# Loading a decode kernel's small inputs as three rows on a second queue, spread by small matrix products

## The chip, the cores and the metric

The kernel runs on one core of one Trainium2 chip. Times are microseconds (us) of device time. An execution's time is about 1.8 us longer than the span in its profile.

Terms: PE is the matrix engine and PEld its weight load; DVE the vector engine, ACT the scalar engine, POOL the GpSimd engine, SP the sync engine. SPq and ACTq are the queues on which SP and ACT issue DMA transfers. The work of a transfer is done by 16 DMA engines, in packets.

## The reference, cut to what matters

```python
x = A_x                                             # [2, 1, 1024], bf16
g = sigmoid((x * gate_w).sum(-1, keepdims=True))    # gate_w: [1024]
q = (x @ wq).reshape(2, 1, 32, 128)                 # wq: 1024 x 4096, 8 MB
a = softmax(q @ k_cache^T / sqrt(128)) @ v_cache    # 2 x 32 heads, 16384 positions, Dh = 128
a = a.reshape(2, 1, 4096) @ wo
b = mixer_mlp(x)                                    # LayerNorm, w1, w2, w3, w4
return g * a + (1 - g) * b
```

The K and V caches are 537 MB of the 572.5 MB that are read. x is 4 KB and gate_w 2 KB.

## The kernel before

Transfers of 8 MB go through three large buffers in the order wq, K0, K1, V0, K2, V1 and so on. A load is issued when the buffer three loads back has been read. So K0 and K1 are issued at once, and V0 when PE has finished with wq. All of them are on SP's queue, x and gate_w behind wq:

```python
    x_pm = const.tile([P, B, KC], BF16)       # P = 128, B = 2, KC = 8
    gw_pm = const.tile([P, KC], BF16)

    def load_first():
        load_rows(["wq"], [A_wq])
        with nc.allow_non_contiguous_dma(reason="a few KB"):
            nc.sync.dma_start(out=x_pm[:], in_=A_x.rearrange("b s (p r) -> p (b s) r", p=P))
            nc.sync.dma_start(out=gw_pm[:], in_=gate_w.rearrange("(p r) -> p r", p=P))
```

In this form a partition gets 8 neighbouring elements of each row, 16 bytes: 256 pieces for x and 128 for gate_w. The query is computed by 64 products, in whose first step x must be in the transposed layout xT:

```python
    def compute_q():
        nc.vector.tensor_copy(out=xT[:], in_=x_pm[:].rearrange("p b r -> p r b"))
        wq = wt.pop("wq")
        ...
                    nc.tensor.matmul(ps[group(g), :], lhsT=xT[:, r, :],
                                     rhs=wq[:, r, c0 : c0 + CW], ...)
        ...
    steps = [("q", compute_q), ("gate", compute_gate)]     # then K0, K1, V0 ...
```

For a K tile, DVE transposes 16 times and PE makes four products after each transpose. The products need z, which is made from q; the transposes do not, but only two of their buffers exist.

## Time and profile before

| | kernel before |
|---|---|
| median of the first 3 executions | 1334.93 us |
| span of the profiled execution | 1333.6 us |
| PE, DVE, ACT busy | 60%, 57%, 2% |
| share of the 16 DMA engines' span taken by SP's queue | 99.4% |

The page of the kernel before, its slices (tenths busy in 40 equal slices of the span) and its queue table (packets, MB, share of 16 engines' span):

```profile
DMA  9999999999999999999999999999999999999998
...
q1 hardware_dynamic: 12729, 572.54, 99.4%
```

The DMA engines are never seen idle for long: q1 is SP's queue, and it fills them. They bound the kernel.

The timeline of the kernel before, its start (start us, us, engine, line, operation, output<-input, count, and in brackets the idle time before it and what ended that):

```profile
0.73 0.38 SPq L159 DMA_DIRECT2D wt<-in_A_wq_dram  x1
1.18 0.41 SPq L185 DMA_DIRECT2D x_pm<-in_A_x_dram  x1
1.63 0.47 SPq L186 DMA_DIRECT2D gw_pm<-in_gate_w_dram  x1
2.14 1.02 SPq L108 DMA_DIRECT2D Kn<-in_A_k_cache_dram  x2
22.81 0.18 DVE L299 COPY xT<-x_pm 128x16 bf16<-128x16 bf16 x1 [19.39 <-DMA x_pm<-in_A_x_dram]
23.04 5.79 PE L311 MATMUL misc<-wt,xT 128*2 128x512 bf16 x64 [19.56 <-DVE xT L299]
28.88 0.33 SPq L119 DMA_DIRECT2D Vn<-in_A_v_cache_dram  x1
43.60 2.37 DVE L369 STREAM_TRANSPOSE T<-Kn 128x1024 f32<-128x1024 f32 x2 [12.45 <-DMA Kn<-in_A_k_cache_dram]
```

Read the brackets. PE stands 19.56 us before the first product and waits for xT, which waits for x, which lies behind wq. The last line shows what follows: once q is done, DVE stands 12.45 us more, because K0 has not landed. It could help only the line before it, V0's issue at 28.88; and V0 has K1 ahead of it in the queue until about 61 us.

### The profile page before, as it was taken

Reading aid. Unit: us, or ns where it says so; the run is one execution under the profiler, and the core shown is the slowest. Engines: PE = TensorE matmul, PEld = TensorE weight load, DVE = VectorE, ACT = ScalarE, POOL = GpSimd, SP = SyncE. Lnnn points to the kernel's source line nnn. Section 1 sums busy time; section 2 is a strip of 40 time slices with the busy share of each in tenths; the row PEclk is TensorE's granted clock in tenths of the full one; section 3 lists DMA queues with packets and bytes.
Section 4 is the critical chain, followed back from the end, with each engine's and each line's share of the span. In section 5 each row is a group of like instructions: output and inputs, shape, how many; then the busy total and the mean of one; then the engine's idle time right before and its main releaser. Section 6 shows DMA issues by size and latency. Waiting matters only on the chain.

```text
span 1333.6 us, 11483 instructions
## 1 busy us (share of the span) xinstructions
PE 797.4 (60%) x4974; PEld 351.3 (26%) x5037; DVE 760.1 (57%) x999; ACT 27.2 (2%) x68; POOL 12.8 (1%) x40
## 2 busy tenths in 40 slices
PE   2576655766556755556665555576655556665564
PEld 0223222322225322222222222232222222222231
DVE  1677665466653665555666555566655556665540
ACT  0000000000000000000000000000000000000000
POOL 0000000000000000000000000000000000000000
PEclk9788777787777777788887777888777788877775
DMA  9999999999999999999999999999999999999998
GB/s 410 437 439 417 439 431 437 423 433 433 438 432 435 429 427 439 439 437 427 429 437 431 439 431 439 429 431 437 429 435 433 439 431 429 435 432 437 429 422 338
DMA packets 12787, 573.27 MB, mean 430 GB/s; under 512 B 1797, under 2 KB 1805, under 8 KB 2613
## 3 DMA queue, kind: packets, MB, share of 16 engines
q1 hardware_dynamic: 12729, 572.54, 99.4%
q8 instruction: 39, 0.64, 0.2%
q14 instruction: 11, 0.09, 0.0%
q10 hardware_dynamic: 8, 0.00, 0.0%
HBM read 572.53 MB, written 0.00 MB: 429 GB/s over the span
## 4 chain that ended last, share of the span: by engine, by line
DVE 30%; PE 30%; DMA 23%; another core or an unknown queue 12%; issue 2%; ACT 1%; SPq 0%; ACTq 0%
DVE T L369 24%; PE S L383 19%; DMA Kn<-in_A_k_cache_dram 13%; PE O L427 7%; DMA wt<-in_B_w_dram 4%; DMA Vn<-in_A_v_cache_dram 3%; DMA wo<-in_A_wo_dram 3%; PE misc L254 2%; DVE Os L442 2%; ACT Pr L411 1%; DVE PT L415 1%; PE misc L585 1%; DVE mx L404 1%; PE misc L566 1%
## 5 line engine op out<-in xcount | busy, mean ns | idle before, releaser
L383 PE MATMUL S<-T,z 128*128 128x512 bf16 x1985 | 579.8, 419 | 330.1 <-DVE T L369 308.5
L369 DVE STREAM_TRANSPOSE T<-Kn 128x1024 f32<-128x1024 f32 x512 | 612.1, 1230 | 255.0 <-DMA Kn<-in_A_k_cache_dram 204.8
L383 PEld LDWEIGHTS <-z 128*128 128x128 bf16 x2048 | 210.0, 104 | 686.6 <-issue 522.8
L427 PE MATMUL O<-Vn,PT 128*32 128x512 bf16 x2048 | 121.4, 390 | 3.6 <-DMA Vn<-in_A_v_cache_dram 3.6
L427 PEld LDWEIGHTS <-PT 128*32 128x32 bf16 x2048 | 73.9, 141 | 49.9 <-issue 20.7
L438 DVE TENSOR_SCALAR Os<-O,xmask 128x128 f32<-128x128 f32 x32 | 11.2, 351 | 101.6 <-PE O L427 101.6
L254 PE MATMUL misc<-rs,ones_f 128*128 128x2 f32 x64 | 17.9, 349 | 79.1 <-DVE rs L458 79.1
L411 ACT ACTIVATE Pr<-S,nb 128x512 bf16<-128x512 f32 x32 | 22.0, 687 | 1199.6 <-DVE nb L406 1161.7
L394 DVE TENSOR_REDUCE m<-S 128x1 f32<-128x512 f32 x32 | 22.2, 693 | 36.9 <-PE S L383 36.9
L450 PE MATMUL misc<-asel,Os 128*128 128x2 f32 x64 | 12.2, 261 | 51.1 <-DVE Os L442 51.1
L415 DVE STREAM_TRANSPOSE PT<-Pr 128x512 bf16<-128x512 bf16 x32 | 22.8, 711 | 28.7 <-ACT Pr L411 28.7
L254 PEld LDWEIGHTS misc<-rs,ones_f 128*128 128x128 f32 x64 | 16.1, 312 | 84.0 <-issue 81.2
L442 DVE SCALAR_TENSOR_TENSOR Os<-O,xmask,Os 128x128 f32<-128x128 f32 x96 | 33.7, 351 | 3.4
L450 PEld LDWEIGHTS misc<-asel,Os 128*128 128x128 f32 x64 | 9.5, 188 | 65.3 <-DVE Os L442 61.0
L254 PE MATMUL misc<-mdiag,ones_f 128*128 128x128 f32 x64 | 15.5, 325 | 17.1 <-DVE mdiag L397 17.1
L404 DVE TENSOR_REDUCE mx<-misc 64x1 f32<-64x64 f32 x64 | 14.2, 222 | 19.1 <-PE misc L254 18.6
L343 POOL TENSOR_TENSOR z<-qsel,own 128x32 bf16<-128x32 bf16 x32 | 10.7, 335 | 1201.2 <-PE S L383 1171.4
L585 PE MATMUL misc<-xn2T,wt 128*128 128x2 bf16 x224 | 14.4, 202 | 7.3 <-DMA wt<-in_B_w_dram 7.3
L462 DVE RECIPROCAL rinv<-misc 128x2 f32<-128x2 f32 x32 | 5.5, 171 | 22.7 <-PE misc L254 22.7
L684 DVE CAST T<-out_acc 128x256 bf16<-128x256 f32 x1 | 0.4, 425 | 30.6 <-PE out_acc L476 30.6
L311 PE MATMUL misc<-wt,xT 128*2 128x512 bf16 x64 | 5.8, 541 | 19.6 <-DVE xT L299 19.6
L585 PEld LDWEIGHTS <-wt 128*128 128x128 bf16 x224 | 14.3, 172 | 7.5 <-DMA wt<-in_B_w_dram 7.5
(86 smaller groups left out, 117.7 us busy)
## 6 DMA issues: line engine op xcount, KB each, us to landing
Vn<-in_A_v_cache_dram SPq DMA_DIRECT2D x2, 4096.0 KB, 41.7
wt<-in_B_w_dram SPq DMA_DIRECT2D x1, 7168.0 KB
w<-in_B_w_dram SPq DMA_DIRECT2D x4, 1792.0 KB, 31.8
wo<-in_A_wo_dram SPq DMA_DIRECT2D x6, 1024.0 KB, 34.1
wt<-in_B_w_dram SPq DMA_DIRECT2D x1, 2048.0 KB, 37.6
wt<-in_B_w_dram SPq DMA_DIRECT2D x1, 1536.0 KB, 41.4
wo<-in_A_wo_dram SPq DMA_DIRECT2D x2, 512.0 KB, 18.8
wo<-in_A_wo_dram SPq DMA_DIRECT2D x4, 256.0 KB, 13.7
```

The lines of the kernel that those rows point to most:

```text
L254: nc.tensor.matmul(ps[:], lhsT=ones_f[:], rhs=src, start=True, stop=True)
L369: moved = nc.vector.transpose(out=T[:].rearrange("p w j s -> p j w s"), in_=Kw[:, m * CW : (m + 1) * CW].rearrange("p (j w e) -> p j w e", ...
L383: nc.tensor.matmul(S[:], lhsT=z[:, v, NM - 1 - m : NM - 1 - m + P], rhs=Tb[:, v // 2, :, v % 2], start=(m == 0 and v == 0), stop=(m == NM ...
L394: nc.vector.reduce_max(out=m[:], in_=S[:], axis=AX.X)
L404: nc.vector.reduce_max(out=mx[pa, :], in_=mall[pa, pa], axis=AX.X)
L411: nc.scalar.activation(out=Pr[:], in_=S[:], func=ACTF.Exp, bias=nb[:], scale=scale, accum_out=rs[:])
L415: nc.vector.transpose(out=PT[:], in_=Pr[:])
L427: nc.tensor.matmul(O[32 * g : 32 * g + 32, :], lhsT=PT[:, m : CJ * 32 : 16], rhs=V[:, j0 : j0 + 4, :], start=(m == 0), stop=(m == NM - 1),)
L442: nc.vector.scalar_tensor_tensor(out=Os[:], in0=Ox, scalar=xmask[:, x : x + 1], in1=Os[:], op0=ALU.mult, op1=ALU.add,)
L450: nc.tensor.matmul(oc[:], lhsT=Os[:], rhs=asel[:], start=True, stop=True)
L566: nc.tensor.matmul(ps[group(g), :], lhsT=actT[rows, r, :], rhs=w[rows, r, g * HW : (g + 1) * HW], start=False, stop=(n == len(slots) - 1), ...
L585: nc.tensor.matmul(ps[:, c, :], lhsT=w[:, r, :].rearrange("k (p c) -> k p c", c=C)[:, :, c], rhs=actT[:, r, :], start=(r == 0), stop=(r == ...
```

## The change

Its intent is to get x and gate_w early: as three long rows on ACT's own queue, not behind wq. A row lies in one partition, so eight small products with an identity spread it over 128 partitions; two DVE copies follow.

```diff
-    x_pm = const.tile([P, B, KC], BF16)
-    gw_pm = const.tile([P, KC], BF16)
+    x_in = []
     def load_first():
+        x_rows = t_tile([B + 1, D], BF16)
+        x_in.append(x_rows)
+        nc.scalar.dma_start(out=x_rows[0:B, :], in_=A_x.rearrange("b s d -> (b s) d"))
+        nc.scalar.dma_start(out=x_rows[B : B + 1, :], in_=gate_w.rearrange("(o d) -> o d", o=1))
         load_rows(["wq"], [A_wq])
-            nc.sync.dma_start(out=x_pm[:], in_=A_x.rearrange("b s (p r) -> p (b s) r", p=P))
-            nc.sync.dma_start(out=gw_pm[:], in_=gate_w.rearrange("(p r) -> p r", p=P))
...
+    def spread_x():
+        x_rows = x_in.pop()
+        xg_ps = misc_psum([P, KC, B + 1])
+        for r in range(KC):
+            nc.tensor.matmul(xg_ps[:, r, :], lhsT=x_rows[:, r:D:KC],
+                             rhs=ident_b[0 : B + 1, 0 : B + 1], start=True, stop=True)
+        nc.vector.tensor_copy(out=xg[:], in_=xg_ps[:])
+        nc.vector.tensor_copy(out=xT[:], in_=xg[:, :, 0:B])
...
-    steps = [("q", compute_q), ("gate", compute_gate)]
+    steps = [("", spread_x), ("q", compute_q), ("gate", compute_gate)]
```

(Cut: the 32-column bf16 identity, the gate's product reading xg, the removed copy in compute_q.)

More of the change, by code (lines that the diff above doesn't have):

```diff
@@ L175, in load_pieces @@
         wt[key] = t
-    x_pm = const.tile([P, B, KC], BF16)
-    gw_pm = const.tile([P, KC], BF16)
+    x_in = []
     def load_first():
+        x_rows = t_tile([B + 1, D], BF16)
+        x_in.append(x_rows)
+        nc.scalar.dma_start(out=x_rows[0:B, :], in_=A_x.rearrange("b s d -> (b s) d"))
+        nc.scalar.dma_start(out=x_rows[B : B + 1, :], in_=gate_w.rearrange("(o d) -> o d", o=1))
         load_rows(["wq"], [A_wq])
-        with nc.allow_non_contiguous_dma(reason="a few KB"):
-            nc.sync.dma_start(out=x_pm[:], in_=A_x.rearrange("b s (p r) -> p (b s) r", p=P))
-            nc.sync.dma_start(out=gw_pm[:], in_=gate_w.rearrange("(p r) -> p r", p=P))
     ident_f = const.tile([P, P], FP32)
@@ L198 @@
     nc.vector.memset(neg_half[:], -0.5)
+    ident_b = const.tile([P, 32], BF16)
+    nc.vector.tensor_copy(out=ident_b[:], in_=ident_f[:, 0:32])
     zero = const.tile([P, 1], BF16)
@@ L259, in over_r @@
         return v.unsqueeze(1).to_broadcast([P, KC, B])
+    xg = const.tile([P, KC, B + 1], FP32)
+    def spread_x():
+        x_rows = x_in.pop()
+        xg_ps = misc_psum([P, KC, B + 1])
+        for r in range(KC):
+            nc.tensor.matmul(
+                xg_ps[:, r, :],
+                lhsT=x_rows[:, r:D:KC],
+                rhs=ident_b[0 : B + 1, 0 : B + 1],
+                start=True,
+                stop=True,
+            )
+        nc.vector.tensor_copy(out=xg[:], in_=xg_ps[:])
+        nc.vector.tensor_copy(out=xT[:], in_=xg[:, :, 0:B])
     g_bc = const.tile([P, B], FP32)
@@ L267, in compute_gate @@
         nc.vector.tensor_tensor(
-            out=prod[:], in0=x_pm[:], in1=gw_pm[:].unsqueeze(1).to_broadcast([P, B, KC]), op=ALU.mult
+            out=prod[:],
+            in0=xg[:, :, 0:B].rearrange("p r b -> p b r"),
+            in1=xg[:, :, B].unsqueeze(1).to_broadcast([P, B, KC]),
+            op=ALU.mult,
         )
@@ L298, in compute_q @@
     def compute_q():
-        nc.vector.tensor_copy(out=xT[:], in_=x_pm[:].rearrange("p b r -> p r b"))
         wq = wt.pop("wq")
```

## The prediction

> **What bounds the kernel now.** The DMA engines. The page's slices show DMA 90% busy or more in 39 of 40; its queue table gives q1 (SyncE's) 99.4% of 16 engines' span for 572.54 MB; PE has 60%, DVE 57%. By the packet records a 64 KB packet takes 2.42 us and the next starts at once, from 1.7 us to about 1317; in the first 1300 us an engine is idle under 3 us in all. Computing waits for data: the groups table puts 204.8 us of DVE idle before the K transposes down to K's DMA.
>
> **The start, from the timeline.** SyncE issues wq at 0.73, x at 1.18, gate_w at 1.63, K0 and K1 from 2.14 us. x lies behind 8 MB of wq on the same rings, so xT is made at 22.81, q's first product runs at 23.04, the q work ends at 31.4; then all stands until K0 lands: DVE waits 12.45 us and starts on K0 at 43.60. V0, which needs wq's buffer, is issued at 28.88, with K1 queued until about 62.
>
> **Removed.** 384 DMA packets of 16 B, in the records in a row between wq and K0, about 9 ns each: 24 an engine, 0.21 us. The gaps between wq's last and K0's first 64 KB packet average 0.21 us too. This is on the critical resource. The wait for x goes as well: q can start when wq lands, at about 22.4 instead of 23.04.
>
> **Added.** Three rows of 2 KB on ScalarE's queue at the start (a 2 KB packet takes 0.085 us here), on the same 16 engines: the Trainium skill ("DMA: Bandwidth & Descriptors", section "Issuing engines are not separate DMA queues") says a second issuing engine interleaves on them and saves only issue time. By the same page's section on why a semaphore rises by 16, two rows use two engines; there I expect 0.1 to 0.2 us. Eight small PE products, a cast and two copies on DVE, roughly 2 us together (the like here take 0.1 to 0.4), at about 4 to 8 us, when PE and DVE have nothing else. ScalarE's table load comes a microsecond later; it is first used at 29.6.
>
> **On the critical path.** Of the earlier q nothing: K0 lands 12 us after the q work, V0 is queued 33 us early. Only the tiny packets' 0.2 us counts, less what the rows cost the slowest engine. wo's last pieces land at 1329.4, the kernel ends at 1333.6; engines finish between 1322 and 1329.4, so 0.1 us on one may vanish. PE gets 16 more instructions; a shifted instruction fetch (39 packets of 16 KB, 0.95 us each) could move the end by some tenths either way.
>
> **Predicted: 1334.7 us (0.2 less), 8 times in 10 between 1333.9 and 1335.5. Faster by over 2%: 0.01; within 2%: 0.98; slower by over 2%: 0.01.**
>
> **Right if** the tiny packets are gone; xT is ready before 8 us; q's first product comes at about 22.4, V0's issue at about 28.3; K0's first transpose moves only 0.2 us, to about 43.4, and DVE's wait before it grows past 13 us; q1 keeps over 99%; the last wo piece lands at about 1329.2.
> **Wrong if** wq's first packets start after 1.7 us because ScalarE's issues come first; wq still lands late; K0 moves over 0.5 us; gaps appear on the DMA engines.
>
> **What would make it wrong.** A start of the DMA queue that the second queue disturbs; an engine that falls behind and sets the end alone; a difference between chips, larger than the effect.

## The result

The changed kernel took 1334.94 us (median of 6, 1334.68 to 1335.15), the kernel before 1334.89 (median of 6, 1334.84 to 1335.04). The ratio is 1.000, with a 95% interval of 0.9987 to 1.0013. Ratios here are the mean time of one kernel's fast runs over that of the other's of the same rounds, so not quite the ratio of the medians.

The page of the changed kernel, the same lines (q10 is ACT's queue):

```profile
DMA  9999999999999999999999999999999999999998
...
q1 hardware_dynamic: 12313, 572.53, 99.4%
...
q10 hardware_dynamic: 14, 0.01, 0.0%
```

q1 lost 416 packets: the 384 of 16 B and their completions. Its share stays at 99.4%. The timeline of the changed kernel, its start:

```profile
0.73 0.39 SPq L159 DMA_DIRECT2D wt<-in_A_wq_dram  x1
0.74 0.56 ACTq L183 DMA_DIRECT2D T<-in_A_x_dram  x1
1.18 1.03 SPq L108 DMA_DIRECT2D Kn<-in_A_k_cache_dram  x2
1.33 0.24 ACTq L184 DMA_DIRECT2D T<-in_gate_w_dram  x1
10.23 0.63 PE L269 MATMUL misc<-ident_b,T 3*128 3x3 bf16 x8 [7.62 <-DMA T<-in_gate_w_dram]
11.12 0.17 DVE L277 CAST xT<-xg 128x16 bf16<-128x16 f32 x1
22.58 6.21 PE L330 MATMUL misc<-wt,xT 128*2 128x512 bf16 x64 [10.53 <-DMA wt<-in_A_wq_dram]
28.85 0.34 SPq L119 DMA_DIRECT2D Vn<-in_A_v_cache_dram  x1
43.22 2.37 DVE L388 STREAM_TRANSPOSE T<-Kn 128x1024 f32<-128x1024 f32 x2 [12.10 <-DMA Kn<-in_A_k_cache_dram]
```

xT is there 11.7 us earlier. PE's wait now ends with wq, not x, and the first product comes 0.46 us earlier. Yet the 64 products take 6.21 us instead of 5.79, and V0's issue has moved by 0.03 us. K0's first transpose has moved by 0.38 us (in a second pair of traces, below, by 0.16: 43.52 and 43.36; so part of it is chance).

Three questions were left. Did the removed packets gain anything? Why did V0's issue not move? And what were the rows and the second queue each for?

### The profile page after: what moved, and what is told of

It reads as the page before. It is cut to its first block, busy times and chain, and to the rows that moved or that the text cites. A ratio compares the mean times of both kernels' runs of the same rounds, so it can differ in the third digit from the quotient of the medians.

```text
span 1333.3 us, 11505 instructions
## 1 busy us (share of the span) xinstructions
PE 805.6 (60%) x4982; PEld 354.5 (27%) x5045; DVE 759.7 (57%) x1001; ACT 27.2 (2%) x68; POOL 12.8 (1%) x40
## 3 DMA queue, kind: packets, MB, share of 16 engines
q1 hardware_dynamic: 12313, 572.53, 99.4%
## 4 chain that ended last, share of the span: by engine, by line
PE 31%; DVE 30%; DMA 23%; another core or an unknown queue 12%; issue 2%; ACT 1%; ACTq 0%; SPq 0%; DVEq 0%
DVE T L388 23%; PE S L402 20%; DMA Kn<-in_A_k_cache_dram 13%; PE O L446 7%; DMA wt<-in_B_w_dram 4%; DMA Vn<-in_A_v_cache_dram 3%; DMA wo<-in_A_wo_dram 3%; PE misc L255 2%; DVE Os L461 2%; ACT Pr L430 1%; DVE PT L434 1%; PE misc L604 1%; PE misc L585 1%; DVE mx L423 1%
## 5 line engine op out<-in xcount | busy, mean ns | idle before, releaser
L469 PE MATMUL misc<-asel,Os 128*128 128x2 f32 x64 | 12.4, 264 | 50.9 <-DVE Os L461 50.9
L484 DVE SCALAR_TENSOR_TENSOR OT<-misc,g_bc,rinv 128x2 bf16<-128x2 f32 x32 | 7.0, 220 | 15.6 <-PE misc L469 15.6
```

What stands on the lines that cost most here:

```text
L469: nc.tensor.matmul(oc[:], lhsT=Os[:], rhs=asel[:], start=True, stop=True)
```

## The experiments

"Its kernel before" is the unchanged kernel on the same chip in the same rounds. Where two times are given as medians and their difference as a mean, the difference is of the means.

### The two kernels once more, and a kernel that loads nothing

The first two kernels are unchanged. The third has no loads of x and gate_w. Its output is wrong, which doesn't matter for the time.

```diff
         load_rows(["wq"], [A_wq])
-            nc.sync.dma_start(out=x_pm[:], in_=...)
-            nc.sync.dma_start(out=gw_pm[:], in_=...)
+        nc.vector.memset(x_pm[:], 0.05)
+        nc.vector.memset(gw_pm[:], 0.05)
```

> The kernel before, unchanged, to see how much two executions of one kernel differ, in time and in the trace. Both theories: ratio 1.000. Theory A (the two traces differ mostly by chance): its start of K0's first transpose lies anywhere from 43.2 to 43.7 us and wq's first packets take anywhere from 2.5 to 3.4 us each, so the 0.38 us by which K0 moved between the two traces is only partly the change. Theory B (the change gained all of it): 43.6 us again, within 0.1.

> The changed kernel again. Theory A (24 packets of 16 B an engine gone, on the resource that bounds all): 0.1 to 0.3 us faster than the kernel before, at the edge of what can be resolved. Theory B (nothing gained at all, the packets fit into time that was free): 0.0. Theory C (the gain is there and is given back at the end): K0's start earlier, the last wo piece not earlier.

> The kernel before with x and gate_w not loaded at all but set to a constant (a wrong result, on purpose): the most that any way of loading them can gain. Theory A: 0.1 to 0.3 us faster, no more than the changed kernel; q's first product at about 22.5 us, V0's issue at about 28.8. The intent of the change (an earlier q is worth something): over 0.5 us faster.

Times: the kernel before again 1335.14 (5 executions, 1334.94 to 1335.93), the changed kernel again 1334.98 (5), without the loads 1334.87 (5), their kernel before 1334.92 (9). So two groups of executions of the very same kernel before, on one chip, differ by 0.30 us in the mean (0.13 without the slowest execution, 1335.93). The changed kernel is 0.04 us below the one group and 0.34 below the other; without the loads it is 0.20 below the first (standard error 0.11). Differences under 0.3 us cannot be told from such times with confidence.

The traces tell more than the times here, because the start has few sources of scatter. From the records of single DMA packets, as means over the 16 engines, in us from the span's start (worked out from the traces; the last column is the one packet of wo that ends last):

```
                     wq's last packet   K0's first   K0's last    wo's last
                     ends               starts       ends         ends
before                    22.01           22.22        41.72       1329.40
before, again             21.93           22.22        41.83       1329.91
changed                   21.94           21.95        41.37       1329.04
changed, again            21.96           21.97        41.39       1329.03
no loads at all           21.91           21.92        41.33       1328.99
```

With the tiny packets there is a gap of 0.21 and 0.29 us between wq and K0, without them none. K0 is complete 0.40 us earlier in the changed kernel (mean of two against mean of two), and the changed kernel reaches what loading nothing reaches, within 0.05 us. Of the 0.40 us, 0.25 is the gap and 0.13 a slower transfer of K0 after it (19.56 against 19.43 us from first to last packet). That it is the packets and not the queue or the rows is supported by x_after_k0 below, where the same packets stand behind K0 on the same queue: K0 is complete at 41.28 (one trace). So the removed packets did cost something, on the resource that bounds, and on an average engine the change recovered it within 0.05 us. wo's column cannot be read in the same way. The two traced executions of the kernel before were among its slowest (1333.6 and 1334.1, where the other executions in these rounds had spans of 1333.0 to 1333.5), and in x_after_k0, which keeps the 24 packets, wo ends at 1328.95, as early as in the changed kernel. Over all executions, on several chips, the changed kernel's mean is 1334.92 (11) and the kernel before's 1335.05 (43): 0.13 us less, give or take 0.13 (two standard errors), but that mixes chips; in the rounds of the result the changed kernel's mean was 0.02 us more (standard error 0.07). So the times do not settle even the sign.

### Why V0's issue did not move: the pace of the products

The timeline of PEld between 22 and 29 us, in the kernel before and then in the changed kernel, cut to where the pace changes. A row holds weight loads that came without a pause; the products are issued four to a group.

```profile
26.83 0.14 PEld L311 LDWEIGHTS <-xT 128*2 128x2 bf16 x4 [0.29 <-issue]
27.26 0.14 PEld L311 LDWEIGHTS <-xT 128*2 128x2 bf16 x4 [0.29 <-issue]
27.58 0.74 PEld L311 LDWEIGHTS <-xT 128*2 128x2 bf16 x16 [0.19 <-issue]
```

```profile
27.23 0.14 PEld L330 LDWEIGHTS <-xT 128*2 128x2 bf16 x4 [0.29 <-issue]
27.66 0.14 PEld L330 LDWEIGHTS <-xT 128*2 128x2 bf16 x4 [0.29 <-issue]
27.98 0.31 PEld L330 LDWEIGHTS <-xT 128*2 128x2 bf16 x8 [0.18 <-issue]
```

Four products take 0.43 us until about 27.5 us in the one and 27.9 us in the other; from then on the pace doubles. The changed kernel started 0.46 us earlier and went slowly 0.4 us longer. The Trainium skill ("TensorE: Matmul & The Clock Gate", section "Part 1: The HAM clock gate") says that an idle PE runs at half its clock until a window of sustained work of about 3.4 us has passed, and that this window runs freely, not from the first product. The traces agree with the free run: in every trace here the stretches between one change of the clock and the next are multiples of 3.41 us, from a start that differs from execution to execution. The first record, for full speed, is at 27.47 and 28.06 us in the two traces of the kernel before and at 27.86 and 27.27 in the two of the changed one, while the first products are at 23.04, 23.06, 22.58 and 22.68. In the 13 traces in which the 64 products run without a pause it comes 3.1 to 5.3 us after the first of them.

A product before the record takes twice the time of one after it, so V0's issue depends half on the first product and half on the record. In 12 of these 13 traces it lies 3.62 to 3.66 us after the middle of the two (in tiny16 SP is busy issuing K1 until 31.2 us, and V0 waits for that). That is the sum for the first pair: 0.46 us of head start count for 0.23, the record that comes 0.40 us later takes 0.20 back, and 0.03 is left. In the second pair (29.18 and 28.60) the record came earlier too, and V0's issue moved by 0.58. So the 0.03 is a chance of the window's phase; half of a head start counts in any case, the other half is won or lost by the phase. The page's PEclk row doesn't show the slow start: in these traces there is no record before the first one, and the row reads full speed.

### The tiny packets behind wq, dosed

To see what a 16 B packet costs, more of them were put behind gate_w in one DMA, read by nobody: 24, 72 and 360 more an engine that read gate_w over and over, and 360 more that read as many different places.

```diff
             nc.sync.dma_start(out=gw_pm[:], in_=gate_w.rearrange("(p r) -> p r", p=P))
+            nc.sync.dma_start(
+                out=t_bufs[0][:, 512:704].bitcast(BF16)[:, 0 : 45 * KC].rearrange("p (n r) -> p n r", n=45),
+                in_=gate_w.rearrange("(p r) -> p r", p=P).unsqueeze(1).to_broadcast([P, 45, KC]),
+            )                       # tiny2: n = 3, tiny4: n = 9
+            # tiny16_far: in_=A_k_cache[0, 0].rearrange("(p j) d -> p j d", p=P)[:, 0:45, 0:KC]
```

> The kernel before with one more DMA of 16 B pieces behind x and gate_w, 15 times as many (5,760 packets, 360 an engine; nobody reads them). Theory A (each costs its engine 9 ns, on the resource that bounds the whole): 15 x 0.21 = 3.2 us slower, K0's first transpose 3.2 us later, and the end 3.2 us later. Theory B (they are hidden by the packets around them, or an early loss is made up later): under 0.5 us slower.

> After the run with 15 times as many 16 B packets came out 12.8 us slower, not 3.2: the kernel before with as many again (48 an engine in all). Theory G (some 60 packets an engine stand ready while wq moves, and these drain at 6 to 9 ns each; only what is beyond them appears at about 38 ns an engine, as seen in that run): 0.2 to 0.4 us slower, K0's first packet on an average engine 0.2 to 0.4 us later than in the kernel before. Theory L (every tiny packet costs 28 ns, the mean of that run): 0.7 us slower.

> The kernel before with three times as many again (96 an engine in all). Theory G: the first 60 or so drain fast, some 36 more at 38 ns: 1.3 to 2.2 us slower, a clear bend against the run with 48. Theory L (28 ns each): 2.0 us slower, with 48 at 0.7. The original step (9 ns each): 0.6 us slower.

> The run with 5,760 more 16 B packets again, but each reads another place (rows of the K cache, 256 B apart) instead of gate_w's bytes over and over. Theory G (the packets are slow because they are made no faster): 11 to 15 us slower, again one packet in about 38 ns an engine in the middle. Theory H (reading the same bytes again was slow): under 5 us slower.

| kernel | more packets an engine | time, median | more than its kernel before (means) | for each packet |
|---|---|---|---|---|
| tiny2 | 24 | 1336.03 | 0.96 us | 40 ns |
| tiny4 | 72 | 1338.67 | 3.45 us | 48 ns |
| tiny16 | 360 | 1347.72 | 12.97 us | 36 ns |
| tiny16_far | 360 | 1338.61 | 3.55 us | 9.9 ns |

tiny16, which ran first, broke the expectation of 3.2 us by four times; tiny2 and tiny4, made to explain it, lay above all of theirs (0.2 to 0.7, and 0.6 to 2.2 us). tiny4's four executions scatter over 2.7 us, so its 48 ns are uncertain by some 8. Theory G, that the packets come no faster than some generator makes them, falls: the same number from different places costs 3.55 us. What was slow was reading gate_w's 2 KB over and over, as theory H said; whether the repeat or the narrow range of addresses makes it slow was not separated. The DMA rows of the two, tiny16 from 22 to 32 us and then tiny16_far from 22 to 25 us (tenths busy in 40 slices of the window, and GB/s):

```profile
DMA  6662111111111111111111249743111121114991
GB/s 18 19 20 9 7 7 7 7 7 7 7 7 7 7 7 7 7 7 7 7 7 7 9 15 28 21 15 12 7 7 6 6 8 7 7 7 72 1054 529 4
```

```profile
DMA  2479999999999999999999999999999999732109
GB/s 6 12 21 29 34 39 43 43 44 43 44 43 44 42 41 40 37 29 35 35 39 39 42 43 43 44 44 43 43 44 41 36 35 29 20 11 6 4 1 2621
```

With different places the engines are 90% busy, packet on packet. With the same place they stand idle most of the time between packets. That a repeated read is slow cost the doses of 24 and 72 their worth as a scale, for they repeat too. What stands is the last row: 9.9 ns for a packet, 24 of them 0.24 us. That is the prediction's term (9 ns, 0.21 us) within its error, and at the dose of 360 it is kept to the end of the kernel: K0 is complete at 45.26, some 3.5 us later than in the kernel before, and 3.55 came out at the end. For 24 packets this is an estimate from the larger dose.

### When q comes: x put later

Here the loads of x are only moved back in SP's queue, by 20 and by 40 us.

```diff
     def load_k(i):
         ...
         kn_tiles[i] = t
+        if i == 0:          # x_after_k1: if i == 1
+            load_x()        # the two loads, taken out of load_first
```

> The kernel before with the loads of x and gate_w put behind K0, 20 us later: q's first product at about 43 us, V0 issued at about 49 instead of 29. Theory A (q's start is off the critical path and has slack, since the DMA queue holds K1 until 62): under 0.5 us slower. The rival (the early q bounds the stages of K0): some 8 us slower, as much as the end of the q work moves past K0's landing.

> The kernel before with the loads of x and gate_w put behind K0 and K1, 40 us later: q's first product at about 63 us, V0 issued at about 69. Theory A (what counts is whether the DMA queue runs dry): it stands idle from about 62 to 70 us, and again a little before V1 and V2 are issued; 8 to 18 us slower, with gaps on the DMA engines up to about 120 us and none after. If q had slack without end: same time.

Behind K0, the timeline has xT and V0's issue 20 us later:

```profile
43.24 0.13 DVE L302 COPY xT<-x_pm 128x16 bf16<-128x16 bf16 x1
48.69 0.34 SPq L121 DMA_DIRECT2D Vn<-in_A_v_cache_dram  x1
```

V0 is issued at 48.69 instead of 28.88 and the time is 1334.93 against 1334.92 (the means differ by 0.10, standard error 0.17): a q that comes 20 us later costs nothing that can be seen. Behind K1, the time is 1347.96 against 1334.92. The windows of that kernel, four stretches of its start (stretch; its length, busy us and count of PE, PEld, DVE, ACT and POOL; granted clock; DMA share; GB/s):

```profile
50.00:60.00 10.00, 0.00 (x0) 0.00 (x0) 0.00 (x0) 0.00 (x0) 0.00 (x0) 1.00 0.97 419
60.00:70.00 10.00, 6.44 (x99) 2.91 (x101) 4.35 (x12) 0.17 (x1) 0.33 (x1) 1.00 0.33 107
70.00:100.00 30.00, 26.07 (x112) 9.55 (x113) 29.32 (x31) 0.78 (x2) 0.33 (x1) 1.00 0.99 420
100.00:110.00 10.00, 9.94 (x59) 3.52 (x58) 9.09 (x9) 0.00 (x0) 0.00 (x0) 1.00 0.74 316
```

The kernel before, the same stretch from 60 to 70 us:

```profile
60.00:70.00 10.00, 5.33 (x21) 2.27 (x20) 6.41 (x12) 0.78 (x2) 0.33 (x1) 0.92 0.98 426
```

K1 has landed by about 61 us, V0 is issued at 66.98, and in between the DMA engines have nothing: their share is 0.33 instead of 0.98. A second gap comes before V1's issue at 110. In the packet records the idle time added in the first 150 us is 10.4 us an engine, and packets after a gap are longer (some 2 us in sum). Together that is the 12.4 us by which the two traced spans differ (1346.0 and 1333.6); the time is 13.3 us more by the means. So the moment of q matters only where it makes the queue run dry, and between the kernel before and that there are at least 20 us. On this scale the change moved q by half a microsecond, on the harmless side.

### The parts of the change: order, queue, rows

Only the order, then only the queue, with the tiny packets kept:

```diff
     def load_first():
-        load_rows(["wq"], [A_wq])
         with nc.allow_non_contiguous_dma(reason="a few KB"):
-            nc.sync.dma_start(out=x_pm[:], ...)
-            nc.sync.dma_start(out=gw_pm[:], ...)
+            nc.sync.dma_start(out=x_pm[:], ...)      # tiny_on_act: nc.scalar
+            nc.sync.dma_start(out=gw_pm[:], ...)     # tiny_on_act: nc.scalar
+        load_rows(["wq"], [A_wq])
```

> The kernel before with the same tiny loads of x and gate_w put ahead of wq on the same queue: the early q without the rows, the second queue and the products. Theory A: same time as before within 0.2 us, because the packets are still there; xT ready at about 3.5 us (earlier than in the changed kernel), q's first product at about 22.7. The intent of the change: as fast as the changed kernel or faster.

> The kernel before with its 384 tiny packets kept and only the queue changed to ScalarE's: the half of the change without the rows. In the changed kernel gate_w's row (one packet and one completion) waited on its engine for one 64 KB packet of wq each. Theory T (the engine takes turns, one packet of each queue): 16 packets of x on an engine wait for about as many 64 KB packets, so xT comes at about 35 to 45 us instead of 22.8, gate_w's at 50 to 65, K0's stage starts well after 43 us, and the time is 1 to 9 us longer. The rival (a turn drains all the tiny packets that stand ready): xT before 10 us and the time as that of the changed kernel, within 0.3 us.

x ahead of wq on the same queue took 1335.80 against 1334.92, 0.9 us more, where I had expected no difference. The timeline of that kernel shows why:

```profile
0.73 0.44 SPq L183 DMA_DIRECT2D x_pm<-in_A_x_dram  x1
1.24 0.45 SPq L184 DMA_DIRECT2D gw_pm<-in_gate_w_dram  x1
1.73 0.43 SPq L159 DMA_DIRECT2D wt<-in_A_wq_dram  x1
2.65 0.17 DVE L298 COPY xT<-x_pm 128x16 bf16<-128x16 bf16 x1 [0.64 <-DMA x_pm<-in_A_x_dram]
23.56 5.32 PE L310 MATMUL misc<-wt,xT 128*2 128x512 bf16 x64 [18.51 <-DMA wt<-in_A_wq_dram]
```

xT is ready at 2.65 us, the earliest of all kernels here, and it is worth nothing. But SP issues wq 1.00 us later, because it issues two other transfers first; wq's first packet starts at 2.80 instead of 1.74 us and K0 is complete at 42.44 instead of 41.72. What counts at the start is the first large packet.

The queue alone took 1354.78 against 1335.09, 19.7 us more. The timeline of that kernel:

```profile
0.74 0.47 ACTq L183 DMA_DIRECT2D x_pm<-in_A_x_dram  x1
1.25 0.48 ACTq L184 DMA_DIRECT2D gw_pm<-in_gate_w_dram  x1
41.94 0.17 DVE L298 COPY xT<-x_pm 128x16 bf16<-128x16 bf16 x1 [39.94 <-DMA x_pm<-in_A_x_dram]
61.45 0.17 DVE L266 TENSOR_TENSOR prod<-x_pm,gw_pm 128x16 f32<-128x16 bf16 x1 [19.34 <-DMA gw_pm<-in_gate_w_dram]
63.18 5.56 PE L310 MATMUL misc<-wt,xT 128*2 128x512 bf16 x64
68.79 0.33 SPq L119 DMA_DIRECT2D Vn<-in_A_v_cache_dram  x1
```

Six KB take until 61 us. The Trainium skill ("DMA: Bandwidth & Descriptors", section "Queues, rings and completion order") says that each DMA engine takes turns between the queues that have work for it, packet by packet. The trace agrees: from 5 us on, 32 to 48 of the 384 tiny packets start in every 5 us on 16 engines, about one an engine in the 2.42 us of each 64 KB packet. 16 packets and a completion, then 8 and a completion, are 26 turns: 63 us by that sum, and 61 measured. DVE keeps to its order in this trace: the gate's product, which waits for gate_w until 61.45, holds up the rest of the setup (perm, which PE needs first, is made at 61.82) and with it q. V0 is issued at 68.79 and the queue runs dry, as in the kernel with x behind K1, but longer: the idle time added in the first 150 us is 17.0 us an engine instead of 10.4. Theory T was right about the turns and too low about the time (1 to 9 us), because I had not counted what stands behind that product.

The changed kernel shows the same rule with few packets. Its x rows started at 1.69 and 1.73 us, ahead of wq. The gate_w row came 0.6 us later, too late: its data packet started at 7.26 us and its completion at 9.76, one 64 KB packet later. The wait before the data packet is longer than one turn, and why is open. The rows without the second queue, put ahead of wq on SP's queue, were not run.

### Smaller packets in the other queue

The changed kernel with wq in four transfers, so that a packet is 16 KB:

```diff
-        load_rows(["wq"], [A_wq])
+        load_pieces("wq", A_wq, [2] * 4)      # load_pieces made to take any row length
```

> The changed kernel with wq loaded as four DMAs of two rows each, so packets of 16 KB instead of 64 KB. Theory A: gate_w's row, which in the changed kernel waited for two packets of 64 KB on its engine (landing seen at about 10 us), waits for packets of 0.6 us and xT is ready before 5 us; the first q product comes when the first quarter of wq lands, at about 7 to 8 us; V0 is issued at 24 to 26 instead of 28.85; and the time stays the same within 0.3 us, since the DMA queue is full in any case.

xT came at 7.54 us (expected before 5): gate_w's completion again came one packet after its data (0.69 us), but the data packet itself started only at 5.52, 3.8 us after wq's first packet, where a packet takes 0.63; turns of one packet do not explain that. q's first product at 7.95, V0's issue at 24.44. The time was 1334.70 (4 executions, 1334.53 to 1334.74) against 1334.92. It is the lowest here, 0.31 us below its kernel before by the means (standard error 0.08). K0 is complete at 41.39 us, 0.39 earlier than in the kernel before and no earlier than in the changed kernel, whose times do not show such a gain. So the 0.31 us may be the tiny packets' gain or scatter; it is no more than the groups of one kernel differ by, and stays open. An early V0 issue, 4.4 us earlier than before, gained nothing that can be told from scatter.

## Why the prediction was right

The time, 1334.94, is in the range and 0.24 us above the number. The range also holds the kernel before (1334.89), so the time alone confirms only that nothing large changed; the 0.2 us forecast did not show in it. What the prediction had right is the mechanism. Point by point:

- **What bounds:** right. With the queue full, a q 20 us later cost nothing (x_after_k0); with the queue dry, the time grew by the gap (x_after_k1).
- **24 tiny packets an engine, 9 ns each, 0.2 us, on the critical resource:** right in kind, and near in size. 360 more from different places cost 9.9 ns each, to the end; in the traces the gap before K0 was 0.21 and 0.29 us, and K0 is complete 0.40 us earlier, about twice the term. In the times it is not resolved.
- **The rows cost 0.1 to 0.2 us on two engines:** not settled. On average over the engines K0 is complete as early as with no loads at all, within 0.05 us, but 0.1 to 0.2 us on two of 16 engines would move that mean by only 0.01 to 0.03. K0's last packet of all ends at 42.66 and 42.80 us, against 42.53 without loads (one trace) and 43.14 and 43.05 before, so a cost of that size on the slowest engine fits.
- **Of the earlier q nothing counts:** right.
- **V0's issue at 28.3:** wrong, 28.85 and 28.60. The step took the products' duration as fixed; it depends on when PE's clock opens (the products took 6.21 and 5.88 us, against the 5.79 that the prediction read from the trace before).
- **DVE's wait before K0 past 13 us:** wrong for the same reason, 12.10 and 12.49: q's work on DVE ended only 0.03 and 0.3 us earlier than in the trace before, and K0 came earlier.
- **xT before 8 us:** wrong, 11.12. The step "on the same 16 engines, saves only issue time" left out that a packet of the second queue waits for a 64 KB packet.
- **First q product at 22.4:** 22.58 and 22.68, near. **The last wo piece at 1329.2:** 1329.04 and 1329.03 in the changed kernel's traces.
- **A start that the second queue delays:** did not happen; wq's first packet started at 1.76 and 1.75 us.

## What to carry to other kernels

Where the DMA engines never rest, a transfer that lands sooner gains nothing unless the queue would have run dry; count what the change takes off the engines or off the issue of the first large packet, and ignore idle brackets of the computing engines. Here a small input on a second queue advanced by one packet for each packet of the large transfer beside it (tiny_on_act), so give it few long packets, or issue it early enough to be ahead. To read differences of a tenth of a microsecond, compare a landmark in the trace that few things disturb, and run the unchanged kernel a second time to see the scatter.

## What the Trainium skill lacked or had wrong

- "DMA: Bandwidth & Descriptors", section "Queues, rings and completion order": it says a turn is a packet of typically 9 to 17 descriptors. Here a turn was a single 16 B piece, and the completion took a turn of its own; the page does not draw the consequence, that 6 KB in 384 pieces beside 64 KB packets took 61 us.
- The same page, "Issuing engines are not separate DMA queues": the issue time that a second engine saves is called usually small relative to the DMA itself. So it was, 1.0 us against wq's 20, and yet 0.9 us of it reached the end where it delayed the first large transfer (x_first).
- The same page says a source may repeat (a broadcast) and gives no cost: 16 B pieces read again and again from the same 2 KB cost 36 to 48 ns an engine each, from different places 9.9 ns.
- "TensorE: Matmul & The Clock Gate": it puts the warm-up around 4 us after sustained work begins, within 0.5 us. Here it came 3.1 to 5.3 us after the first product in 13 traces, a wider scatter, which the page's own free-running window leads one to expect at the upper end; 3.1 is a little less than the 3.4 us of one window.
